# Paced loads in the first loop of an RWKV-6 and GELU kernel: second-step loads, one weight block and one ACT step are moved

## The chip, the cores and the metric

The kernel runs on one core of a Trainium2 chip. The metric is the device time of one execution in microseconds (us). Before the change three runs took 575.78, 577.08 and 580.18 us; the median is 577.08 us. The engines are TensorE (PE, with PEld for its weight loads), VectorE (DVE), ScalarE (ACT), GpSimd (POOL) and SyncE (SP), which here only issues DMAs.

## The reference

RWKV-6 attention on 4 batches, 8 heads, 768 steps and head size 48, then an exact GELU MLP on the 3072 x 384 result.

```python
for t in range(S):                       # S = 768, state is 48 x 48 per head
    kt, vt, rt, wt = (k[:, :, t], v[:, :, t], r[:, :, t], w[:, :, t])
    cur = np.einsum('bhd,bhe->bhde', u[None] * kt, vt)
    y[:, :, t] = np.einsum('bhd,bhde->bhe', rt, state + cur)
    state = wt[:, :, :, None] * state + np.einsum('bhd,bhe->bhde', kt, vt)
x = y.transpose(0, 2, 1, 3).reshape(3072, 384)
h = x @ w_in                             # 384 x 2048
g = 0.5 * h * (1.0 + erf(h / sqrt(2)))
return g @ w_out                         # 2048 x 384
```

## The kernel before

The work is cut into eight steps x = 0 to 7, each half the sequence (384 time steps) of one batch with all heads. Attention is done in chunks of 64 time steps: products of k and r at doubling distances ("levels" h = 1, 2, 4 to 32) are masked into the matrix `a_sb`, then `kv` products make the states, then `a_sb` times v plus r times the states gives y, which is packed into `xT`. Part of y goes into `xT` by copies of ACT and DVE, part is copied to `ysb` by ACT and moved into `xT` by six small DMAs, three issued by SP and three by ACT (`pack`, L886). The MLP of a step runs while the attention of the next step is prepared, so PE has products of both in its queue. The MLP of step 0 (`first_mlp`, L1079 to L1100) makes 16 blocks f of h = x w_in, three matmuls each, in two PSUM banks in turn; ACT applies the GELU to each block (L1086) and so frees its bank.

The weights arrive as 64-bit floats and are converted on the chip in sixteen blocks, eight of w_in and eight of w_out, each 768 KB: `prepare` does three ACT steps on the raw words (L459, L460, L462), `finish` two DVE steps (L471, L475). `weight_in` loads a block, either in one DMA (L322) or, with `gate`, in thirds (L327). Each gated DMA is preceded by a DVE memset of one column of its target, so that it can't be issued before DVE has come to that point in its queue. `conversion` also issues the load of the block three further on, ungated. `load_second` loads r, k and w of step 1 in eight gated shares of 288 KB (L285, L286), r first, w last. `load_first` loads step 0's r, k, w in six DMAs of 384 KB at the start (L274), and `load_v` follows with v, 584 KB (L278).

The order of the instructions on each engine is the order in which the program issues them: nothing is rescheduled. It is written out by hand in `PLAN`. Each letter of `PLAN[x]` advances one stream by one step. In `PLAN[0]`, which covers the first 40 us or so, "." and "s" are the two halves (units) of step 0's attention, "f" is the attention of step 1, "c" the conversions, "l" the gated loads, "w" the load of v of step 1, "p" two further `prepare`s and "x" three matmuls on zeros that keep PE occupied (`warm`). All loads go through SP's queue in program order. In step 1's attention, the first "f" multiplies u and r on ACT (L524, four activations) and makes the running products of w on DVE (L534); the next one issues the first products on PE (L575).

Of the kernel before, what the change touches and what calls it, by code (L numbers as in the profile page):

```python
# [10 lines left out]
F32 = mybir.dt.float32  # L11
# [25 lines left out]
NC_SP = 8  # L37
HALFWAY = 2
PLAN = {
    0: "l.s....llsl.lssslslss.lc.l.slslls...ssss..lcs.s.s.l.ss..ss..sccs.c.s.llpssslw..cs.ffpccxx",  # L40
    1: (
        "swcs.clc.cs.wccscwcc.csccsw..cwlsccccccsc.cs.swcccc.ccc.s.cwlssccsclcs.cwss.lscccsw.c.cwcw"
        ".s..clw..lw..wwccc..cccc.scc.l.cslfccscfccw.fcffy.w.y..fw....ywyw..yyxxx.wyfxx..x.w..y.fyx"
# [149 lines left out]
def kernel(  # L193
# [9 lines left out]
    nc = tc.nc  # L203
# [12 lines left out]
    io = ctx.enter_context(tc.tile_pool(name="io", bufs=2))  # L216
# [8 lines left out]
    def pair(name):  # L225
        return pools["d"].tile([128, 2, BANK], F32, name=name, tag="d")
# [14 lines left out]
    def bank(name="o_ps", i=None):  # L241
        if i is None:
            i = turns[0]
            turns[0] = 1 - i
        return ps.tile([128, BANK], F32, name=name, tag=f"m{i}")
# [4 lines left out]
    loaded = {}  # L250

    def units_of(x):
        return NPART if x == 0 else 1
# [4 lines left out]
    bufs = [io.tile([128, 3 * NP * T], F32, name=f"rkw{i}", bufs=1) for i in range(2)]  # L258
# [7 lines left out]
    def load_first():  # L266

        t = bufs[0]
        loaded[0] = [None, None]
        size = 3 * NP * T // units_of(0)  # L270
        nc.scalar.dma_start(out=u_sb, in_=u)
        for i, part in ((0, 2), (0, 0), (0, 1), (1, 0), (1, 1), (1, 2)):
            s = slice(i * size + part * size // 3, i * size + (part + 1) * size // 3)
            nc.sync.dma_start(out=t[:, s], in_=rkw[0, :, s])  # L274

    def load_v(x, dma):
        loaded[x][1] = io.tile([128, v.shape[2]], F32, name="v_in", bufs=1)
        dma.dma_start(out=loaded[x][1], in_=v[x])  # L278

    def load_second(dma):  # L280

        loaded[1] = [None, None]
        for i in range(SHARES):
            s = slice(i * 3 * ALL // SHARES, (i + 1) * 3 * ALL // SHARES)
            nc.vector.memset(bufs[1][:, s.start:s.start + 1], 0.0)  # L285
            dma.dma_start(out=bufs[1][:, s], in_=rkw[1, :, s])  # L286
            yield
# [26 lines left out]
    def weight_in(i, gate=False):  # L314

        if i < len(pieces):
            dst, src = pieces[i]
            raws[i] = cv.tile([128, PIECE], I64, name="raw", bufs=AHEAD) if wide else None
            if wide:
                dst = raws[i].rearrange("p (a c) -> p a c", a=dst.shape[1])  # L320
            if not gate:
                nc.sync.dma_start(out=dst, in_=src)  # L322
                return
            for a in range(dst.shape[1]):
                if wide:
                    nc.vector.memset(dst[:, a].bitcast(U32)[:, 0:1], 0)
                nc.sync.dma_start(out=dst[:, a], in_=src[:, a])  # L327
                yield

    load_first()  # L330
    load_v(0, nc.sync)


    zeros = const.tile([128, BANK], BF16, name="zeros")
# [8 lines left out]
    def keep_warm(n, elsewhere=False, n_cols=BANK):  # L343
        if elsewhere:
            t = pair("warm")[:, 0]
        else:
            t = bank("warm")
        for _ in range(n):
            nc.tensor.matmul(t[:, 0:n_cols], lhsT=zeros[:, 0:128], rhs=zeros[:, 0:n_cols], start=True, stop=True)
# [83 lines left out]
    def conversion():  # L433

        i = converted[0]
        if i >= len(pieces):
            return
        converted[0] += 1

        prepare(i + HALFWAY if i > 1 else 0)  # L440
        yield
        if wide:
            yield from finish(pieces[i][0], raws[i], *halfway[i])
        for _ in weight_in(i + 3):
            pass

    def convert():
        for _ in conversion():
            pass

    def prepare(upto):
        if not wide:
            return
        for i in range(len(halfway), min(upto, len(pieces))):
            words = raws[i].bitcast(U32).rearrange("p (a b) -> p a b", b=2)
            lo, hi = words[:, :, 0], words[:, :, 1]
            f = cv.tile([128, PIECE], U32, name="f")
            e = cv.tile([128, PIECE], U32, name="e")
            nc.scalar.activation(out=f.bitcast(F32), in_=hi.bitcast(F32), func=AF.Abs, scale=2.0 ** -112)  # L459
            nc.scalar.activation(out=e.bitcast(F32), in_=lo, func=AF.Identity, scale=2.0 ** -51, bias=two)  # L460
            sign = e.bitcast(F16).rearrange("p (a b) -> p a b", b=2)[:, :, 1]
            nc.scalar.activation(out=sign, in_=hi.bitcast(F32), func=AF.Copy, scale=2.0 ** -100)  # L462
            halfway.append((f, e))

    def finish(dst, raw, f, e):

        nc.vector.tensor_scalar(out=f, in0=f, scalar1=3, scalar2=None, op0=ALU.logical_shift_left)  # L471
        yield
        yield
        f, e = (z.rearrange("p (a c) -> p a c", a=dst.shape[1]) for z in (f, e))
        nc.vector.tensor_tensor(out=dst.bitcast(U32), in0=f, in1=e, op=ALU.add)  # L475
# [3 lines left out]
    def attention(x, unit):  # L479
# [20 lines left out]
        def transposed_sums(o, e, n):  # L500
            nc.vector.tensor_reduce(out=fine_sb[:, e, 0:n].rearrange("p a n -> p (a n)"),  # L501
                                    in_=kx[:, o:o + n * n_m].rearrange("p (m j) -> p m j", j=32),
                                    axis=mybir.AxisListType.X, op=ALU.add, apply_transpose=True)
# [7 lines left out]
        if x >= 2:  # L511
            for q in range(qs):
                m_q = slice(q * T // FINE, (q + 1) * T // FINE)
                nc.vector.scalar_tensor_tensor(out=kx[:, 0:n_u].rearrange("p (a m) -> p m a", a=FINE)[:, m_q],
                                               in0=r4[:, m_q], scalar=u_sb[:, q:q + 1], in1=k4[:, m_q],
                                               op0=ALU.mult, op1=ALU.mult)
            yield
            transposed_sums(0, 0, FINE)
            yield
        else:  # L520

            rus = [kx[:, b * Q * T:(b + 1) * Q * T] for b in parts]
            for q in range(qs):
                nc.scalar.activation(out=rus[q // Q][:, q % Q * T:(q % Q + 1) * T], in_=r[:, q * T:(q + 1) * T], func=AF.Copy,  # L524
                                     scale=u_sb[:, q0 + q:q0 + q + 1])
            rucs = [ru.rearrange("p (i c t) -> p i c t", c=2, t=C) for ru in rus]


# [381 lines left out]
        else:  # L910
# [22 lines left out]
            for turn in range(2):  # L933
                ysb = ysb_of() if turn == 0 else ysb
                a = ys[turn][1][:, :, 0:NI * C].rearrange("p b (q i t) -> p b q i t", q=Q, t=C)
                for z in range(2):
                    s = slice(z * G, z * G + D)
# [9 lines left out]
        if split:  # L947
            for c, copy in enumerate((nc.scalar.copy, nc.vector.tensor_copy)):
                for z in range(2):
                    s = slice(z * G, z * G + D)  # L950
                    copy(out=xT[s, 0:Q, :].rearrange("p q (i c t) -> p (q i) c t", c=2, t=C)[:, :, c, :],
                         in_=ys[0][0][c][s, 0:NI * C].rearrange("p (i t) -> p i t", t=C))
# [3 lines left out]
        for b in reversed(range(np_)):  # L956
            for q in reversed(range(Q)):
# [5 lines left out]
                if which < NJ:  # L963
                    for z in range(2):
                        s = slice(z * G, z * G + D)
# [274 lines left out]
    second = load_second(nc.sync)  # L1240
# [8 lines left out]
    def prepare_apart():  # L1249
        for i in range(2, 2 + HALFWAY):  # L1250
            prepare(i)
            yield

    def next_v():
        load_v(1, nc.sync)
        yield

    def warm():
        for _ in range(2):
            keep_warm(3, True)  # L1260
            yield

    def masks_and_sums():
        yield from make_quarter_masks()
        homes()
        yield from h_sums([0])
# [3 lines left out]
    for x in range(NX):  # L1270
        following = attention(x + 1, 0) if x + 1 < NX else iter(())
        if x == 0:
            streams = {
                ".": units[0], "s": units[1], "f": following, "c": pieces_of_w, "w": next_v(), "x": warm(),
                "p": prepare_apart(),
                "l": chain(weight_in(0, True), islice(second, 5), weight_in(1, True), second, weight_in(2, True)),
            }
        else:
            streams = {
                **(mlp(x - 1) if x > 1 else {".": first_mlp()}),  # L1280
                "s": slots, "f": following,
                "l": load(x + 1, nc.sync),
                "x": sums_of_x(x),
                "w": masks_and_sums() if x == 1 else chain(h_sums([1]), o_sums(EARLY, len(FORMS_O))) if x == 2 else iter(()),
                "y": o_sums(0, EARLY) if x == 1 else iter(()),
                "c": pieces_of_w if x == 1 else iter(()),
            }
        for c in PLAN[x]:
            next(streams[c], None)
        for c in ".slxwp" if x == 0 else ".slxwcy" if x == 1 else ".vgeoslxw":  # L1290
            while next(streams[c], streams) is not streams:
                pass
        slots = following
        if x == 1:
            fewer_pairs()
# [63 lines left out]
```

## Time and profile before

| | before |
|---|---|
| median of three runs | 577.08 us |
| the profiled execution | 577.52 us |
| its span | 575.7 us |
| granted TensorE clock | 1.00 |
| PE, DVE, ACT, POOL busy | 551.3, 489.2, 334.1, 106.1 us |
| packets of the queue for instructions (q8) | 58, 0.95 MB |

The span runs from the first to the last instruction on the engines; 1.8 us of the execution lie around it. The first part of the page gives the busy time of each engine, the second cuts the span into 40 slices of 14.4 us with the busy share in tenths. In the order of time, a line gives the start, the duration, the engine, the line of the code, the output and its inputs, the count, and in brackets the idle time of the engine before it and what ended it. "issue" stands where the profile shows nothing that was waited for. SPq and ACTq are DMA issues; their duration is that of issuing. A line's matmul count is twice the program's, since a 32-bit matmul makes two records.

### The profile page before, as it was taken

How to read it: one execution, taken by the hardware profiler on the slowest of the kernel's cores; microseconds unless marked ns; L12 is line 12 of the kernel's file. 1: busy time of each engine (PE TensorE's matmuls, PEld its weight loads, DVE VectorE, ACT ScalarE, POOL GpSimd, SP SyncE). 2: the span in 40 equal slices, each digit the busy share in tenths (PEclk: the TensorE clock that was granted, in tenths of full speed). 3: DMA queues.
4: the chain of work that ended last, by engine and by line, in shares of the span. 5: the costliest groups of instructions: out<-in, count | busy, mean ns of one | idle time of the engine just before them, and what ended most of it. 6: DMA issues, size and time to landing. Idle time of an engine off the chain costs nothing. (4 is left out here: it accounts for less than half of the span.)

```text
span 575.7 us, 17712 instructions
## 1 busy us (share of the span) xinstructions
PE 551.3 (96%) x7412; PEld 491.1 (85%) x7420; DVE 489.2 (85%) x977; ACT 334.1 (58%) x768; POOL 106.1 (18%) x105
## 2 busy tenths in 40 slices
PE   7689999999998999999999999999999999999997
PEld 4576665689998989999898998989898988999997
DVE  7889879999989989798989979799888989755464
ACT  2468995347753677347763477527772478535820
POOL 5100000016200460006400252005500072000000
PEclk9999999999999999999999999999999999999999
DMA  8559742239342782558623593337915384200001
GB/s 303 178 159 370 239 142 87 81 86 154 47 82 64 175 106 36 139 156 131 81 46 114 135 165 44 60 91 159 131 30 135 84 105 62 43 25 30 0 1 41
DMA packets 71646, 62.15 MB, mean 108 GB/s; under 512 B 32912, under 2 KB 56720, under 8 KB 71568
## 3 DMA queue, kind: packets, MB, share of 16 engines
q1 hardware_dynamic: 50112, 45.62, 26.4%
q0 software_dynamic: 21216, 15.34, 20.3%
q8 instruction: 58, 0.95, 0.7%
q14 instruction: 20, 0.16, 0.1%
q10 hardware_dynamic: 240, 0.08, 0.1%
HBM read 36.24 MB, written 4.72 MB: 71 GB/s over the span
## 5 line engine op out<-in xcount | busy, mean ns | idle before, releaser
L1148 POOL DMA_DIRECT2D g<-o_sb x78 | 94.9, 1490 | 370.7 <-ACT g L1117 347.2
L1197 DVE TENSOR_TENSOR g<-g 128x512 f32<-128x512 f32 x112 | 75.1, 688 | 24.3 <-PE o_ps L1073 21.3
L1117 ACT COPY o_sb<-u_ps 128x384 f32<-128x384 f32 (+1 forms) x56 | 25.8, 461 | 67.6 <-PE u_ps L1073 66.2
L1073 PE MATMUL h_ps<-forms_x,w_in_sb 128*128 128x192 f32 x280 | 57.7, 332 | 0.0
L1073 PE MATMUL o_ps<-w_out_sb,g 128*128 128x192 f32 x280 | 50.5, 327 | 0.5 <-DVE g L1197 0.5
L1117 ACT COPY g<-h_ps 128x384 f32<-128x384 f32 x84 | 40.4, 482 | 16.3 <-PE h_ps L1073 14.4
L1073 PEld LDWEIGHTS h_ps<-forms_x,w_in_sb 128*128 128x128 f32 x280 | 46.6, 190 | 2.7 <-ACT g L1117 2.2
L1073 PEld LDWEIGHTS o_ps<-w_out_sb,g 128*128 128x128 f32 x280 | 46.0, 190 | 1.2 <-DVE g L1197 0.8
L1166 ACT ACTIVATE g<-g 128x384 f32<-128x384 f32 x98 | 46.2, 519 | 0.3
L1073 PE MATMUL o_ps<-t,g 128*128 128x192 f32 x224 | 41.4, 328 | 0.1
L726 ACT COPY a_sb<-d 32x320 f32<-32x320 f32 (+5 forms) x108 | 39.3, 364 | 3.6 <-DVE a_sb L784 1.7
L1073 PEld LDWEIGHTS o_ps<-t,g 128*128 128x128 f32 x224 | 36.8, 190 | 0.7 <-PE u_ps L1073 0.3
L1073 PE MATMUL h_ps<-forms_x,s 128*128 128x192 f32 x168 | 35.5, 334 | 0.0
L1073 PE MATMUL h_ps<-xT,w_in_sb 128*128 128x192 f32 x168 | 35.0, 331 | 0.1
L710 PE MATMUL d<-kx,rkw 64*64 64x96 f32 x1152 | 32.0, 248 | 3.0 <-ACT a_sb L726 1.9
L710 PEld LDWEIGHTS d<-kx,rkw 64*64 64x64 f32 x1152 | 25.6, 133 | 9.6 <-issue 4.3
L1084 PE MATMUL h_ps<-xT,w_in_sb 128*128 128x384 f32 x96 | 33.0, 494 | 0.2
L1073 PE MATMUL u_ps<-xT,w_in_sb 128*128 128x192 f32 x168 | 32.5, 328 | 0.1
L1073 PE MATMUL u_ps<-w_out_sb,g 128*128 128x192 f32 x168 | 30.9, 332 | 1.4 <-ACT o_sb L1115 0.8
L1092 PE MATMUL o_ps<-w_out_sb,g 128*128 128x384 f32 x96 | 31.7, 489 | 0.0
L575 PEld LDWEIGHTS d<-rkw 64*64 64x64 f32 x1152 | 19.1, 134 | 14.2 <-issue 8.5
L739 DVE COPY_PREDICATED a_sb<-quarter,d 128x480 f32<-128x480 uint8 (+5 forms) x54 | 23.2, 440 | 8.7 <-PE d L710 7.4
(178 smaller groups left out, 1206.2 us busy)
## 6 DMA issues: line engine op xcount, KB each, us to landing
g<-o_sb POOLq DMA_DIRECT2D x78, 192.0 KB, 4.2
rkw<-in_rkw_dram SPq DMA_DIRECT2D x54, 256.0 KB, 3.7
raw<-in_w_out_dram SPq DMA_DIRECT2D x8, 768.0 KB, 5.4
v_in<-in_v_dram SPq DMA_DIRECT2D x8, 584.0 KB, 4.6
out_dram<-o_sb SPq DMA_DIRECT2D x24, 192.0 KB, 2.1
raw<-in_w_in_dram SPq DMA_DIRECT2D x5, 768.0 KB, 9.2
rkw<-kx SPq DMA_DIRECT2D x72, 48.0 KB, 2.1
rkw<-in_rkw_dram SPq DMA_DIRECT2D x6, 384.0 KB, 6.8
```

The lines of the kernel that those rows point to most:

```text
L575: nc.tensor.matmul(d[half[p], g, n * width:(n + 1) * width], lhsT=kc[half[g], b, i, p], rhs=right(half[g], b, i, p), start=True, stop=True)
L710: nc.tensor.matmul(d[half[p], g, i * 3 * C // 2:(i + 1) * 3 * C // 2], lhsT=kc[half[g], n // NI, n % NI, p], rhs=rx[half[g], 2 * n + p], s ...
L726: nc.scalar.copy(out=at[z, g, first:behind, (a + 1) * h:], in_=d[z, :, :, to] if g == slice(None) else d[z, :, to])
L739: nc.vector.copy_predicated(out=an[:, :, :, :, (a + 1) * h:], mask=mask.to_broadcast(data.shape), data=data)
L1073: nc.tensor.matmul(o, lhsT=lhsT, rhs=rhs, start=start, stop=True, skip_group_check=True)
L1084: nc.tensor.matmul(h_ps, lhsT=w_in_sb[:, f // FI, j, f % FI * 128:(f % FI + 1) * 128], rhs=xT[:, j, :], start=(j == 0), stop=(j == NJ - 1))
L1092: nc.tensor.matmul(o, lhsT=gs[f // FG][:, f % FG, i * 128:(i + 1) * 128], rhs=w_out_sb[:, f, :], start=(f == 0), stop=(f == NF - 1))
L1117: nc.scalar.copy(out=o, in_=z)
L1148: nc.gpsimd.dma_start(out=o, in_=saved[q, t], accum_op=ALU.add)
L1166: nc.scalar.activation(out=o, in_=z, func=AF.Gelu, scale=MINUS.get(h, 1.0))
L1197: nc.vector.tensor_add(o, o, g_block(what[3:5]))
```

## The change

Only the first loop's program changes. The order of PE's matmuls stays. What moves is this:

- v of step 0 is no longer loaded by `load_v` ahead of everything; it is loaded in two gated halves (`first_v`), after w_in's block 0.
- `PLAN[0]` has 20 steps of "l" instead of 17, at other places. The gated order was: block 0, five shares of step 1, block 1, three shares, block 2. It is now: block 0, the two halves of v, five shares, block 1, three shares, block 2, block 3. The last three shares come after the first fence on y, where they came among the products of the levels. All three thirds of block 2 now stand behind the DMAs of `ysb` in SP's queue, with the load of step 1's v between the first and the second; two of them were ahead of these DMAs.
- w_in's fourth block (block 3) is no longer issued in one DMA by the first `conversion`; it is loaded in gated thirds at the end of the list.
- In step 1's attention, u times r gets a step of its own (`if x: yield`), and the plan's extra "f" places it on ACT's queue ahead of the copy to `ysb` and its DMAs. It followed the copies into `xT`.
- The matmuls of `warm` in the first loop have 64 columns instead of 512.

```diff
-    0: "l.s....llsl.lssslslss.lc.l.slslls...ssss..lcs.s.s.l.ss..ss..sccs.c.s.llpssslw..cs.ffpccxx",
+    0: ".s....ls.lssslslss.lc.l.slss.l..lsssls..lcs.s.sl..lss..ss..sccs.c.s.psslfllslw..lcs.llffpccxx",
...
+    def first_v():
+        loaded[0][1] = t = io.tile([128, v.shape[2]], F32, name="v_in", bufs=1)
+        for i in range(2):
+            s = slice(i * v.shape[2] // 2, (i + 1) * v.shape[2] // 2)
+            nc.vector.memset(t[:, s.start:s.start + 1], 0.0)
+            nc.sync.dma_start(out=t[:, s], in_=v[0][:, s])
+            yield
+
     load_first()
-    load_v(0, nc.sync)
...
             yield from finish(pieces[i][0], raws[i], *halfway[i])
-        for _ in weight_in(i + 3):
+        for _ in weight_in(i + 3) if i else ():
             pass
...
                                      scale=u_sb[:, q0 + q:q0 + q + 1])
+            if x:
+                yield
             rucs = [ru.rearrange("p (i c t) -> p i c t", c=2, t=C) for ru in rus]
...
         for _ in range(2):
-            keep_warm(3, True)
+            keep_warm(3, True, 64)
             yield
...
-                "l": chain(weight_in(0, True), islice(second, 5), weight_in(1, True), second, weight_in(2, True)),
+                "l": chain(weight_in(0, True), first_v(), islice(second, 5), weight_in(1, True), second, weight_in(2, True), weight_in(3, True)),
```

## The prediction

> **What bounds the kernel now.** I read the page's first two parts, then the order of time from 0 to 125 us, because nothing after that changes its order of instructions.
>
> ```profile
> PE 551.3 (96%) x7412; PEld 491.1 (85%) x7420; DVE 489.2 (85%) x977; ACT 334.1 (58%) x768; POOL 106.1 (18%) x105
> PE   7689999999998999999999999999999999999997
> q8 instruction: 58, 0.95, 0.7%
> ```
>
> TensorE (PE) is full but for the first three slices, 43 us. That is the first loop, which the change rewrites. 7412 + 7420 = 14,832 PE records over 58 instruction packets are 256 to a packet, so the packets of q8 feed PE's program. That matters here:
>
> ```profile
> 18.12 0.45 PE L575 MATMUL d<-rkw 64*64 64x64 f32 x11 [1.46 <-issue]
> 18.66 0.96 DVE L628 TENSOR_TENSOR rkw<-rkw,tot_sb 128x768 f32<-128x768 f32 x1 [0.45 <-issue]
> 20.03 0.96 DVE L628 TENSOR_TENSOR rkw<-rkw,tot_sb 128x768 f32<-128x768 f32 x1 [0.41 <-PE d L575]
> 22.68 1.39 PE L575 MATMUL d<-rkw 64*64 64x64 f32 x80 [0.61 <-issue]
> 27.45 1.20 DVE L617 TENSOR_TENSOR rkw<-rkw,tot_sb 128x384 f32<-128x384 f32 x2 [0.84 <-issue]
> 33.98 0.86 PE L865 MATMUL y_ps<-a_sb,v_in 64*64 64x64 f32 x44 [1.39 <-issue]
> 37.71 1.59 PE L575 MATMUL d<-rkw 64*64 64x32 f32 x94 [0.57 <-issue]
> ```
>
> The pauses marked "issue" stand in the middle of a run of equal matmuls, where no operand can be missing. Counting PE's records, PE resumes after them at numbers 447, 701, 955, 1211, 1723 and 1979, that is 254 to 256 apart or twice that: it is out of instructions. The times of these boundaries (13.19, 18.12, 22.68, 26.41, 30.25, 33.98, 37.71, 41.31 us) give what one packet takes: 4.93 and 4.56 us from 13 to 23 us, while loads ran at 185 to 270 GB/s (the table by stretches of 4 us), and 3.6 to 3.8 us afterwards, at 43 to 262 GB/s. So traffic may explain part of it, not all. VectorE (DVE) is 88% busy from 10 to 30 us and loses to PE only the 0.45, 0.41 and 0.84 us above and 0.15 us at 23.43: 1.85 us.
>
> ```profile
> 36.10 0.48 ACT L970 COPY ysb<-y_ps 128x384 f32<-128x384 f32 x1 [1.79 <-PE y_ps L894]
> 36.60 1.86 SPq L886 DMA_DIRECT2D xT<-ysb  x3
> 38.57 0.56 SPq L327 DMA_DIRECT2D raw<-in_w_in_dram  x1
> 39.23 1.23 SPq L278 DMA_DIRECT2D v_in<-in_v_dram  x1
> 39.87 2.14 ACT L524 ACTIVATE kx<-rkw,u_sb 128x384 f32<-128x384 f32 x4
> 42.17 0.93 ACT L459 ACTIVATE f<-raw 128x768 f32<-128x768 f32 x1 [0.15 <-DMA raw<-in_w_in_dram]
> 42.58 6.07 PE L1084 MATMUL h_ps<-xT,w_in_sb 128*128 128x384 f32 x18
> 45.15 0.49 ACT L1086 ACTIVATE g<-h_ps 128x384 f32<-128x384 f32 x1
> 48.58 1.60 PE L575 MATMUL d<-rkw 64*64 64x32 f32 x96
> 50.48 0.93 ACT L459 ACTIVATE f<-raw 128x768 f32<-128x768 f32 x1 [1.30 <-DVE w_in_sb L475]
> ```
>
> The hand-over to the second loop: the packed copy ysb, its DMAs into xT, u times r, then the MLP's h products f0, f1, f2 (each 6.07/3 = 2.02 us), for which ScalarE (ACT) converts w_in block by block (about 3 us each). From 42.58 to 120 us PE has no idle time before any group but fractions of a us, so **whatever delays PE after 42.6 us is kept to the end.** ACT sits in front of it: 9.4 to 9.9 of each 10 us busy from 50 to 90. The gelu of f0 stands on ACT behind the three conversions of block 2 (42.17 to 45.13), and f2 needs the PSUM bank which that gelu frees at 45.64. PE reached f2 at 42.58 + 4.05 = 46.6: **1.0 us to spare.**
>
> **The change part by part.**
>
> *Loads of 8 to 30 us.* v no longer goes ungated behind the first six loads; block 0's thirds are gated after the first updates (about 9, 11 and 12.4 us), v's halves follow at about 14.5 and 15.5, five shares of the second r,k,w until 23, block 1 until 26.6. The last three shares and the old 768 KB load at 27.04 leave this stretch. Seven more memsets of 0.06 us on DVE, partly under their neighbours: 0.1 us. Gain: the first two packets could come in 3.7 instead of 4.9 and 4.6 us; in the other direction, block 1 and the shares now run at 22 to 27 us, where the packet took 3.73. Ends: 1.85 us won (all of DVE's waits) and 0.4 us lost. I take 0.4 won, near the small end, since the bytes are moved within the stretch more than taken out of it, and traffic alone didn't set the packet's time. The Trainium skill, "Runtime: NRT & Kernel Launch", section "Instruction fetch mechanics", says that the program streams in 16 KiB blocks of 256 instructions and that crossing a block is mostly hidden; the block size agrees with the trace, the hiding doesn't (1.46 and 1.39 us). By that sentence this part would win nothing, and the sum below would be 0.4 us higher.
>
> *The gap around kv (27 to 33 us).* Packets there took 3.73 to 3.84 us under load and 3.6 without: 0.1 to 0.2 us each, nothing.
>
> *The last three shares.* Their memsets now stand behind the first y fence (33.23 us before), so they are issued at about 33.3 to 34.3; a 288 KB share took 3.7 us at least to land. The first is due for the second part's products (36.9 before), the others for DVE's tot at 38.92. 37.0 to 38.3: just in time, 0 to 0.3 us.
>
> *u times r ahead of ysb.* Four activations, 2.14 us. ACT is free at 34.30 (end of L462), idle for 1.79 us until 36.10. 34.30 + 2.14 = 36.44, so ysb comes 0.34 us later, less the 0.4 won above: 36.0 to 36.4. xT's DMAs, and DVE's L967, which waits for ysb, move with it. With this, u times r is ready when the products want it; the six warm matmuls go from 512 to 64 columns, about 1.3 of their 1.47 us. Together f0 could start up to 1.6 us earlier, if instructions arrive (next boundary 41.31) and xT has landed: 36.6 + 3.4 to 4.8 us.
>
> *Block 2 after xT.* This is where I see the end set. Before, two thirds of block 2 were issued at 31.20 and 31.63, and one at 38.57. Now its first third goes out after xT's six small DMAs, then v of the second part, then the other two. The compiled lists of both kernels show that each DMA takes the next of eight completion counters and its issue waits until that counter's last DMA has landed. In the changed list the second third waits for ACT's first xT DMA and the last third for SP's first. These start at 36.6 and take 3.4 to 4.4 us, so the last third goes out at about 40.6, not 38.57. Landing, bound below: a 256 KB third took 3.5 us from 38.57 with an empty queue, so 44.1. Bound above: it queues behind v, 584 KB, which landed at 44.96 before, and another 1 us of its own: 46.0. I take 45.2, the middle, as v is in front but partly drained. ACT then starts block 2 at 45.2, not 42.17; u times r being out of its way gives it nothing but idle time. Gelu of f0 ends at 45.2 + (45.64 - 42.17) = 48.7, and f2 starts at 48.7, not 46.6: **+2.1 us** (+1.0 to +2.9 by the bounds), whenever f0 started. f3 follows after 2.02 + 1.6 us at 52.3; it needs the gelu of f1, behind block 3 on ACT: 45.2 + 6.6 = 51.8, no further wait. On ACT, block 4 starts at 45.2 + 7.0 = 52.2 against 50.48.
>
> *Block 3 in thirds at the end.* It was loaded at 27.04; now behind block 2, two thirds gated by memsets after DVE's L471 (41.5). Three thirds at 0.7 to 1.0 us each after 45.2 land at 47.5 to 48.2; ACT wants it at 48.7. Covered by block 2's own lateness; without that cover it would cost 2 us by itself, as ACT wanted it at 45.54. All later loads come 1.3 MB later in a queue that moved 390 GB/s from 47 to 53: 3.4 us. Block 4 then lands at about 49 against 52.2, w_out blocks have 7 us (converted 91, used 99). Nothing.
>
> **Sum.** The early gains end in the wait for f2, so they don't add: +2.1 us. The profiled execution took 577.52 us (span 575.7), so 579.6; the runs' median is 0.44 lower, so I write **579.3**.
>
> **The rivals.**
> 1. *The early gain is carried.* If the last third of block 2 lands by 43.1 us (46.6 - 3.47), f2 waits for nothing, and 0.5 to 1.5 us of the early stretch remain: 576.1. For it: 1.5 us of packet pauses and 1.79 us of ACT idle. Against: the counter would have to be free at 39.5, when xT has been under way for 3 us. Chance 0.23.
> 2. *Nothing moves.* Early gain 1 us and block 2 at 44 cancel, within 0.7 us of before: 577.1. Chance 0.15.
> 3. *Slower, and more.* Block 3's last thirds fall behind v and block 2, and ACT waits for them too: block 3 at 50 instead of 48.7 adds 1.3 us, and DVE, whose L471 for block 2 stands in order ahead of the mask copies that free d's buffers, adds up to 1 us: 581.5. Decides from a landing at 49 us. Chance 0.13.
> 4. *The clock.* PE would idle from about 45.7 to 48.7. The longest gap in this trace is 1.5 us, at a granted clock of 1.00 throughout. If it fell to half for the next 3.4 us, that would add 1.7 us: 581.0. "TensorE: Matmul & The Clock Gate" of the Trainium skill, part 1, tells of half clock after an idle window of about 3.4 us; no run here shows it. Chance 0.04.
>
> The forecast itself has 0.45. The range takes in rivals 1 to 4 but for their tails: 575.0 to 582.0. One per cent, 5.8 us, is about what a measurement of this kernel can tell from no change; no case reaches it alone, so within 1% has 0.93, faster 0.02, slower 0.05.
>
> **What would show it.** In the new profile: ACT's first conversion after xT's copies waits for DMA raw until 44 to 46; the first h_ps group on PE breaks after two products, with an idle time before the third released by ACT g; the x11 and x44 groups' pauses shrink, if pacing works; ysb starts at 36.0 to 36.5. I am wrong if block 2 lands by 43, or if PE's idle time after 60 us swallows 2 us.

## The result and the profile after

The changed kernel took 580.3 us (median of 22 runs, 576.26 to 585.59), the kernel before 577.3 us in 22 runs beside them: ratio 1.0046, 95% interval 1.0026 to 1.0066. (The ratio is worked out over the fast runs and is not the quotient of the two medians, which here is 1.0052.) The forecast was 579.3 in a range of 575.0 to 582.0, within 1%. So the number held. The way to it held in part: one step came out on the spot, one that I called nothing was not, and what the rival with the smallest chance names, the clock at half speed, was at work in most executions (15 of 22).

The profiled execution of the changed kernel took 578.78 us, its span 577.0, at a granted clock of 1.00. The first two parts of its page:

```profile
PE 550.2 (95%) x7420; PEld 490.3 (85%) x7420; DVE 489.4 (85%) x982; ACT 332.8 (58%) x768; POOL 106.0 (18%) x105
...
PE   7769999999998999999999999999999999999997
```

PE did 1.1 us less work than before (the six warm matmuls went from 1.47 to 0.35 us) in a span 1.3 us longer. From the order of time, the lines of PE and DVE that answer to the pauses before (all line numbers are 7 to 9 higher than before):

```profile
16.18 0.45 PE L584 MATMUL d<-rkw 64*64 64x64 f32 x11 [0.68 <-issue]
...
20.85 1.40 PE L584 MATMUL d<-rkw 64*64 64x64 f32 x80 [0.68 <-issue]
...
25.90 1.20 DVE L626 TENSOR_TENSOR rkw<-rkw,tot_sb 128x384 f32<-128x384 f32 x2 [1.10 <-issue]
...
30.07 0.62 PE L833 MATMUL kv_ps<-v_in,kx 64*64 64x48 f32 x28 [1.19 <-issue]
...
33.52 0.86 PE L874 MATMUL y_ps<-a_sb,v_in 64*64 64x64 f32 x44 [1.36 <-issue]
...
38.07 1.60 PE L584 MATMUL d<-rkw 64*64 64x32 f32 x94 [1.26 <-issue]
...
42.07 1.26 PE L584 MATMUL d<-kx,rkw 64*64 64x64 f32 x68 [1.47 <-issue]
```

The x11 group starts at 16.18, not 18.12, after 0.68 us of waiting instead of 1.46: the early part is faster. But a new pause stands in the middle of the kv products (x28), the pause before x94 has doubled (0.57 before), and x68 ahead of f0 waits for its program too. The hand-over:

```profile
32.63 2.11 ACT L531 ACTIVATE kx<-rkw,u_sb 128x384 f32<-128x384 f32 x4
...
35.64 0.48 ACT L979 COPY ysb<-y_ps 128x384 f32<-128x384 f32 x1 [0.90 <-PE y_ps L903]
...
43.27 4.14 PE L1093 MATMUL h_ps<-xT,w_in_sb 128*128 128x384 f32 x12
...
45.08 0.91 ACT L466 ACTIVATE f<-raw 128x768 f32<-128x768 f32 x1 [5.72 <-DMA raw<-in_w_in_dram]
...
48.02 0.49 ACT L1095 ACTIVATE g<-h_ps 128x384 f32<-128x384 f32 x1
...
48.56 2.20 PE L1093 MATMUL h_ps<-xT,w_in_sb 128*128 128x384 f32 x6 [1.15 <-ACT g L1095]
...
50.69 1.60 PE L584 MATMUL d<-rkw 64*64 64x32 f32 x96
...
52.06 0.92 ACT L466 ACTIVATE f<-raw 128x768 f32<-128x768 f32 x1
```

ACT waits 5.72 us for block 2 and starts it at 45.08; the gelu of f0 follows at 48.02, and f2 (the x6 group) at 48.56, where it was at 46.6 before. The x96 group stands at 50.69 against 48.58: PE is 2.11 us behind. Aligned instruction by instruction, it is still 2.0 us behind at 77 us, 1.59 at 83 us, 1.1 around 400 us and 1.57 in the last products.

**A second thing the runs say.** Each run gives its mean granted clock, and that falls in steps of 0.003: one step is a stretch of 3.41 us at half clock. The profiled executions of both kernels have none of these. The 22 runs of the changed kernel have 1.64 per execution (none in 7 of 22, three in 9), the 92 runs of the kernel before that stand beside the experiments 0.45 (none in 63). A straight line through each kernel's runs gives

| | runs | mean us | stretches per execution | line: us without any + us per stretch |
|---|---|---|---|---|
| before | 92 | 578.1 | 0.45 | 577.3 + 1.78 |
| changed | 22 | 580.5 | 1.64 | 578.1 + 1.45 |

So of the 2.4 us between the means about 0.8 is there at full clock; 1.19 more stretches at 1.45 to 1.78 us are 1.7 to 2.1 us. (The two make a little more than the whole, since the lines are fitted.) The 0.8 is rough: by the scatter of the runs about the lines its standard error is 0.6 us. The 92 runs were taken in four groups, whose own lines start at 576.8 to 577.6 us. And the 22 runs of before that stand beside the changed ones have a mean of 577.5, 3.0 us lower; there is no clock for each of them.

### The profile page after: what moved, and what is told of

The parts are those of the page before. It is cut to its first block, busy times and chain, and to the rows that moved or that the text cites. A ratio compares the mean times of both kernels' runs of the same rounds, so it can differ in the third digit from the quotient of the medians.

```text
span 577.0 us, 17734 instructions
## 1 busy us (share of the span) xinstructions
PE 550.2 (95%) x7420; PEld 490.3 (85%) x7420; DVE 489.4 (85%) x982; ACT 332.8 (58%) x768; POOL 106.0 (18%) x105
## 3 DMA queue, kind: packets, MB, share of 16 engines
q1 hardware_dynamic: 50288, 45.62, 26.7%
## 5 line engine op out<-in xcount | busy, mean ns | idle before, releaser
L1206 DVE TENSOR_TENSOR g<-g 128x512 f32<-128x512 f32 x112 | 75.0, 687 | 24.3 <-PE o_ps L1082 21.4
L1082 PEld LDWEIGHTS h_ps<-forms_x,w_in_sb 128*128 128x128 f32 x280 | 46.6, 190 | 2.7 <-ACT g L1126 2.1
```

Source lines behind the costliest of these rows:

```text
L1082: nc.tensor.matmul(o, lhsT=lhsT, rhs=rhs, start=start, stop=True, skip_group_check=True)
L1206: nc.vector.tensor_add(o, o, g_block(what[3:5]))
```

## The experiments

Two theories at first. A: the late block 2, as forecast, makes the loss. B: the stretches at half clock make most of it. In the last column a line as above; it is left out where it is not steady. Its standard error is 0.4 to 1.1 us, so two kernels that differ there by less than 1 us can't be told apart by it.

| kernel | runs | median | ratio to before | stretches | line at none |
|---|---|---|---|---|---|
| changed | 22 | 580.3 | 1.0046 [1.0026, 1.0066] | 1.64 | 578.1 |
| e1: changed, warm 512 | 12 | 580.5 | 1.0044 [1.0022, 1.0066] | 0.67 | 579.4 |
| e2: changed, block 2 early | 11 | 581.1 | 1.0042 [1.0017, 1.0068] | 1.36 | |
| e3: before, warm 64 | 12 | 577.7 | 1.0008 [0.9979, 1.0037] | 1.17 | 577.0 |
| e4: before, block 2 late | 7 | 583.4 | 1.0081 [1.0045, 1.0116] | 2.14 | |
| e5: changed, v last | 8 | 581.0 | 1.0063 [1.0037, 1.0088] | 1.12 | 578.7 |
| e6: changed, blocks in time, warm 512 | 12 | 579.9 | 1.0046 [1.0023, 1.0069] | 0.83 | 578.5 |
| e7: before, u times r ahead | 12 | 577.9 | 1.0015 [0.9990, 1.0041] | 0.67 | 576.5 |
| e8: before, early loads paced | 6 | 580.5 | 1.0072 [1.0043, 1.0101] | 1.50 | 578.8 |
| e9: changed, 14 matmuls on zeros | 6 | 586.1 | 1.0104 [1.0059, 1.0149] | 1.50 | 584.2 |
| e10: e7, 14 matmuls on zeros | 12 | 583.2 | 1.0069 [1.0038, 1.0100] | 0.67 | 581.9 |
| e11: before, block 3 late | 12 | 578.9 | 0.9995 [0.9964, 1.0026] | 0.58 | 577.9 |
| e12: e8 and e11 together | 10 | 580.1 | 1.0046 [1.0024, 1.0068] | 0.90 | 580.0 |

### e1 and e3: the width of the warm matmuls

```diff
-            keep_warm(3, True, 64)      # e1, in the changed kernel
+            keep_warm(3, True)
-            keep_warm(3, True)          # e3, in the kernel before
+            keep_warm(3, True, 64)
```

> The changed kernel with one part undone: the six warm matmuls of the first loop have 512 columns again. Theory A (the time is lost to the late landing of w_in's block 2, and nothing else): nothing gained, since PE waits for its program at 42.07 anyway; ratio to before as for the changed kernel, 1.003 to 1.007, ACT's first conversion after the xT copies again at about 45. Theory B (in many executions TensorE's granted clock falls, because PE has too little to do between 36 and 48 us; the executions of the changed kernel had mean clocks of 0.990 to 1.000, those at 0.991 took about 582 us, those at 1.000 about 578): with 1.3 us more PE work just there the low clocks become rare, and the median falls from 580.3 to about 578.5, ratio about 1.002.

> The kernel before with one part of the change alone: warm matmuls of 64 columns. Theory A: nothing, ratio 0.999 to 1.001, since u times r (39.87 to 42.01) sets the start of the products and not PE. Theory B: PE is idle for 1.3 us more from 39.6, so low clocks (0.991 to 0.997) appear in part of the executions and the ratio is 1.002 to 1.005.

Both ways the narrow matmuls go with more stretches (0.67 to 1.64, 0.45 to 1.17). The line at none is lower with them (579.4 to 578.1, 577.3 to 577.0), but not by more than its errors allow. The ratios don't move: 1.0044 beside 1.0046, and 1.0008 beside 1. So theory A's ratios were met and theory B's were not, though the counts went B's way. Whether the matmuls on zeros save or cost time can't be told from these runs.

In the traces the busy share of PE over 3.41 us falls, between 36 and 43 us, to no less than 0.82 (before) and 0.70 (e1), but to 0.57 (changed) and 0.56 (e3) with 64 columns. None of these four profiles lost the clock there, though. The one stretch at half clock in e3's profile runs from 13.5 to 16.9 us, where its program is still that of before; e10 and e11, which have the loads of before too, lost theirs at the same place. Only e5, with 64 columns, lost it after 36.4 to 39.8 us. That the width brings stretches on is therefore what the counts say; the traces of e1 and e3 don't show it.

### e2 and e4: block 2 early in the changed kernel, late in the one before

```diff
-        for _ in weight_in(i + 3) if i else ():           # e2
+        for _ in weight_in(i + 3 if i else 2):
...
-..., second, weight_in(2, True), weight_in(3, True)),
+..., second, weight_in(3, True)),
...
-... "ssss..lcs.s.s.l.ss..ss..sccs.c.s.llpssslw..cs.ffpccxx",      # e4
+... "ssss..lcs.s.s.l.ss..ss..sccs.c.s.pssslwll..cs.ffpccxx",
```

In e2 block 2 is loaded in one DMA by the first conversion at 25 us. In e4 all its thirds go behind the DMAs of `ysb`, the last two behind v, and nothing else changes.

> The changed kernel, but the first conversion issues the load of block 2 (768 KB, one DMA, at about 25.5 us, where the kernel before issued block 3), and only block 3 is loaded in thirds behind ysb's DMAs. Theory A: ACT converts block 2 as soon as it has copied xT (about 39.5), f2 follows f1 without a wait, and the 2.1 us on PE at 48.6 are gone; ratio 0.997 to 1.001, a fast profile's span 575 to 576. Theory B alone: the warm matmuls are still short, but the wait for f2 is gone, so fewer low clocks than in the changed kernel. A rival, that the load in the gap slows the program's packets around kv: the pauses before kv and y (1.19 and 1.36 us) grow by 0.5 us each or more, and the ratio stays above 1.002.

> The kernel before with one part alone: all three thirds of block 2 stand behind ysb's DMAs on SP, with v between the first and the second, as in the changed kernel; block 3 stays in one DMA at 27 us. Theory A: block 2 lands at 45 to 46, f2 starts 2 to 2.8 us later than before (46.6), the ACT chain 1.6 to 2.2 us later, ratio 1.003 to 1.004, span 577.3 to 578. If late landing were harmless, 1.000. Theory B says nothing against that, but adds low clocks if PE's wait for f2 is what lowers them (ratio 1.005 and more).

In e2's order of time, f0 to f2 run through, and the wait has moved on to f3:

```profile
33.94 0.87 PE L874 MATMUL y_ps<-a_sb,v_in 64*64 64x64 f32 x44 [1.91 <-issue]
...
43.61 6.07 PE L1093 MATMUL h_ps<-xT,w_in_sb 128*128 128x384 f32 x18
...
49.13 0.92 ACT L466 ACTIVATE f<-raw 128x768 f32<-128x768 f32 x1 [2.80 <-DMA raw<-in_w_in_dram]
...
52.44 6.07 PE L1093 MATMUL h_ps<-xT,w_in_sb 128*128 128x384 f32 x18 [1.23 <-ACT g L1095]
```

Block 3, which the lateness of block 2 had covered, is now what ACT waits for, and f3 starts at 52.44 against 52.22 in the changed kernel. It is not the only reason: f0 itself starts 1.03 us later than before (42.58), since PE waited 1.91 us at y for its program (1.36 in the changed kernel) and then lost the clock from 34.66 to 38.08. Before kv the wait was 0.92, so of the rival's two pauses one grew. Nothing is won: 1.0042, where theory A had 0.997 to 1.001. In e4 the loss is larger than in the change, and than theory A had it (f2 2 to 2.8 us later, 1.003 to 1.004): f2 starts 5.0 us later than before. Of e4, PE's line for f2 in the order of time:

```profile
51.61 4.21 PE L1084 MATMUL h_ps<-xT,w_in_sb 128*128 128x384 f32 x6 [4.14 <-ACT g L1086]
```

and its table by stretches (from and to, us, busy time and count of PE, PEld, DVE, ACT and POOL, granted clock, DMA share, GB/s):

```profile
46.80:50.20 3.40, 0.67 (x3) 0.05 (x1) 1.08 (x2) 1.98 (x3) 0.00 (x0) 1.00 1.04 389
50.20:53.60 3.40, 1.99 (x3) 1.17 (x4) 3.37 (x5) 3.34 (x5) 0.00 (x0) 0.50 1.04 374
53.60:57.00 3.40, 3.40 (x52) 1.93 (x53) 2.37 (x4) 2.20 (x4) 0.00 (x0) 0.50 1.00 360
```

PE is busy for 0.67 of 3.4 us while it waits for block 2 (ACT's first conversion 48.19, 6.0 us later than before), and the next 6.8 us run at half clock. Here one can see theory A's wait become theory B's stretch. Late block 2 alone is therefore enough for a loss; in the changed kernel it was milder (45.08).

### e5: v behind the blocks

```diff
-... "psslfllslw..lcs.llffpccxx",
+... "psslfllsl..lcs.llllwffpccxx",
```

> The changed kernel with one thing moved: the load of step 1's v is issued behind blocks 2 and 3, not between the first and the second third of block 2. Theory A (the landing of block 2 sets the kept loss; v's 584 KB in front of its last two thirds are part of it): the last third lands at 44.0 to 44.5 us, not 45.05, ACT's first conversion of block 2 starts there, and f2 starts at 47.5 to 48.0 after 0.3 to 0.6 us of waiting instead of 1.15; PE is then 1.2 to 1.5 us behind before at 60 us, not 2.1. At full clock about 0.5 to 0.7 us less than the changed kernel. Theory B (the loss seen in the median is mostly 3.41 us windows at half clock, drawn anew in each execution): the same number of such windows as the changed kernel, 1.2 to 2.0 per execution, so that the ratio to before stays at 1.003 to 1.005 and a gain of 0.6 us is hardly seen. If the third waits for the counter of SP's first xT DMA and not for v's transfer, the landing stays at 44.7 to 45.1 and neither moves.

ACT's first conversion of block 2 starts at 44.56, 0.5 us earlier than in the changed kernel, just above the 44.0 to 44.5 expected; v was a part of the lateness, a small one, for with v out of the way the issue of the last third was late (held until about 41 us, by the profile for DVE's tot, and done at 41.29). f2 runs on without a wait, but at 49.42: f0 itself started at 44.30, since this execution had 6.8 us at half clock from 39.82 on. By the ratio nothing is won.

### e6: no wait left at f2 and f3

```diff
-        for _ in weight_in(i + 3) if i else ():
+        for _ in weight_in(i + 3 if i else 2):
...
-            keep_warm(3, True, 64)
+            keep_warm(3, True)
...
-... "psslfllslw..lcs.llffpccxx",
+... "psslfllsl..lcs.llwffpccxx",
```

> The changed kernel with block 2 in one DMA issued by the first conversion (about 25 us), so that it's there long before ACT wants it; block 3 in gated thirds where block 2's thirds were, the load of v behind them; and the warm matmuls at 512 columns again. It keeps the paced early loads and u times r ahead of the copy to ysb. Theory A: neither f2 nor f3 waits; ACT's first conversion of block 2 follows the copies into xT at 40 to 41 us, block 3 lands at 44 to 45 against about 45.5 wanted. PE is 0 to 1 us behind before at 60 us, and the fit at zero windows gives 577.0 to 578.0. The 768 KB of block 2 run at 25 to 28 us, which takes back the gap around kv: the program packet there takes 5 us or more, and DVE's pause at kv stays at 1 to 1.5 us. Theory B: with 512 columns and without the idle time at f2 there are 0.4 to 0.9 windows per execution, so the ratio is 0.999 to 1.002; with 1.2 or more windows theory B's account of what brings them on is wrong.

As expected neither f2 nor f3 waits. Yet f0 starts at 44.86, 2.3 us later than before, and the ratio is 1.0046. Theory B had 0.999 to 1.002 for the 0.83 stretches that it counted rightly. The line at none, 578.5, is above A's 577.0 to 578.0 by less than its error. The loss sits earlier; PE's lines in the order of time:

```profile
25.87 2.84 PE L584 MATMUL d<-rkw 64*64 64x64 f32 x96 [2.11 <-DVE raw L326]
...
32.21 0.62 PE L833 MATMUL kv_ps<-v_in,kx 64*64 64x48 f32 x28 [1.12 <-issue]
...
44.86 6.07 PE L1093 MATMUL h_ps<-xT,w_in_sb 128*128 128x384 f32 x18
```

Between the first two starts lie 6.34 us for one packet of the program. The trace records each of these packets: this one began 3.97 us after PE had entered the last one. Block 2's 768 KB had been issued at 25.43, just ahead of it. And in the stretch of 3.41 us from 22.2, with a busy share of 0.35, the clock was lost for the next one (25.56 to 28.98).

### e7: u times r ahead of the copy, alone

```diff
-... "llpssslw..cs.ffpccxx",
+... "llpssfslw..cs.ffpccxx",
...
+            if x:
+                yield
```

> The kernel before with one part of the change: u times r is a step of its own on ACT, ahead of the copy to ysb. Loads and warm matmuls as before. Forecast by the prediction's step: ACT fills its 1.79 us pause with 2.1 us of activations, ysb starts 0.3 to 0.5 us later (36.4 to 36.6), xT's DMAs land 0.3 to 0.5 us later, f0 starts where it did or 0.3 later (42.6 to 42.9), and PE has up to 1 us to spare before f2, so nothing is kept: ratio 0.999 to 1.001. ACT's first conversion of block 2 moves from 42.17 to about 40.5, so f2 has more to spare. Theory B: windows as before, 0.3 to 0.8 per execution. If this part alone costs 1 us or more, or brings 1.2 windows or more, the late block 2 isn't the only source of the base loss.

1.0015 [0.9990, 1.0041]: no difference that these runs can tell. (The line at none, 576.5, stands beside 576.8 for the runs of before in the same group.) ACT's first conversion of block 2 moved only to 41.24, since it then waits for the data. PE is 0.42 us ahead of before at 60 us, but it is 1.2 ahead already at 18 us, where the two programs are the same: so much do two executions differ by the waits for program packets.

### e8, e11 and e12: paced early loads and the gap around kv, alone and together

```diff
-    0: "l.s....llsl.lssslslss.lc.l.slslls...ssss..lcs.s.s.l.ss..ss..sccs.c.s.llpssslw..cs.ffpccxx",
+    0: ".s....ls.lssslslss.lc.l.slss.l..lsssls..lcs.s.sl..llllss..ss..sccs.c.s.llpssslw..cs.ffpccxx",   # e8
...
+    def first_v(): ...                   # e8, as in the change; load_v(0, nc.sync) goes
...
-        for _ in weight_in(i + 3):       # e11: block 3 in thirds at the end
+        for _ in weight_in(i + 3) if i else ():
```

e12 has both edits.

> The kernel before with only the early loads paced: v of step 0 in two gated halves behind block 0, block 0 later, five shares, block 1, then the last three shares straight after it; block 3 still in one DMA by the first conversion, two thirds of block 2 ahead of ysb's DMAs, 512 columns, u times r where it was. Theory A (the early gain is real but is lost again to program packets and then hidden behind the hand-over): DVE is 1 to 1.8 us ahead of before at 25 us, 0 to 1 us at 38 us, 0 to 0.5 us at 60 us; no wait at f2. At full clock 576.4 to 577.4, ratio 0.998 to 1.000. If the early gain were carried whole, 575.5 and ratio 0.997. Theory B: 0.3 to 0.8 windows per execution, like before, since PE does the same work in nearly the same times.

> The kernel before with block 3 alone moved: from one DMA at the first conversion (27 us) to thirds at the end of the list, behind the load of step 1's v. So it has the gap in the loads around kv, and block 2 lands as before. The prediction's steps: the gap is worth 0.1 to 0.2 us (packets there took 3.73 to 3.84 us under load and 3.6 without), and block 3 late, uncovered, costs about 2 us. By the counters and the transfers in front of it (v of 584 KB and 768 KB of its own) the last third lands at 46.5 to 48.5, and ACT wanted it at 45.54: ACT starts block 3 1.0 to 3.0 us late and PE is that much later at f3, 50.1 + 1 to 3, kept to the end: ratio 1.002 to 1.005. The other theory of the gap, from the version without it (a packet asked for at 28.9 us had to wait for 3.5 us behind loads, where 1.1 is the least): the packets asked for at 26.4 and 30.25 start 1.1 us after their boundary and take 3.45 to 3.6 us, not 3.73 to 3.84; that is no more than 0.4 us in all, since before asks for them where little is queued. Windows 0.3 to 1.0, as PE idles at f3.

> The kernel before with the paced early loads (as in the version that did only that) and block 3 moved from 27 us to thirds at the end of the list, so that the loads pause around kv. Against the version without that move it takes 768 KB out of the queue at 26.7 us. The packet theory (a program packet waits in its DMA engine behind loads issued before it was asked for): there the packet asked for at 28.9 us started 3.47 us later, and PE waited 3.83 us for it; now it starts 1.1 to 2.2 us later, PE waits 1.4 to 2.5 us, ysb starts at 34.8 to 36.0, not 37.7, and f0 at 41.8 to 42.8, not 44.95. If something else held that packet (the three shares issued at 25.3 us, or the program's own place in the order), its start stays 3 us or more behind its boundary. Block 3 then lands at about 48.5 and costs 1 to 2 us at f3, as when it alone was moved (f3 at 52.1). Sum: PE 0.5 to 1.8 us behind the profile of before at 60 us, the fit at zero windows 576.8 to 578.2, windows 0.3 to 0.9, ratio 0.999 to 1.003: the early gain pays for the late block 3 and no more.

e8 fell outside what either theory allowed. At 26 us PE is 1.9 us ahead of before, at 42.6 it is 2.4 behind. PE's lines in the order of time:

```profile
28.88 0.62 PE L831 MATMUL kv_ps<-v_in,kx 64*64 64x48 f32 x28 [0.36 <-issue]
...
34.80 0.86 PE L872 MATMUL y_ps<-a_sb,v_in 64*64 64x64 f32 x44 [3.83 <-issue]
```

and the table by stretches, with the columns as above:

```profile
28.90:32.30 3.40, 2.07 (x128) 1.93 (x128) 2.90 (x19) 3.37 (x4) 0.00 (x0) 1.00 0.92 336
32.40:35.80 3.40, 1.00 (x57) 1.00 (x58) 1.65 (x11) 0.00 (x0) 0.00 (x0) 1.00 0.54 203
35.80:39.20 3.40, 3.40 (x81) 3.40 (x79) 1.07 (x4) 0.48 (x1) 0.00 (x0) 0.50 0.02 5
```

After 28.88 the loads run at 336 GB/s, and the next packet begins only at 32.35, 3.47 us after PE entered the last one: PE is out of program for 3.83 us, and pays again with a stretch at half clock, in which the products with the states take 3.79 us. e12 takes one thing away, the 768 KB of block 3 at 26.7 us, and the pause halves (order of time, PE and ACT):

```profile
33.04 0.86 PE L872 MATMUL y_ps<-a_sb,v_in 64*64 64x64 f32 x44 [1.91 <-issue]
...
35.69 0.48 ACT L977 COPY ysb<-y_ps 128x384 f32<-128x384 f32 x1 [2.88 <-PE y_ps L901]
...
42.18 6.41 PE L1091 MATMUL h_ps<-xT,w_in_sb 128*128 128x384 f32 x18
```

ysb comes at 35.69 instead of 37.73 and f0 at 42.18 instead of 44.95, both in the ranges expected of the packet theory. So the loads were what held the packet. On the loads of before, the same move (e11) leaves the packet as it was: asked for at 26.63, begun at 27.73, 1.10 us later, as before (26.41 and 27.50). In e11 the late block 3 makes f3 wait 1.15 us on PE; the ratio is 0.9995 [0.9964, 1.0026], an interval that has room for 1.15 us (0.2%), so the runs neither show this loss nor exclude it.

e12's sum failed: 1.0046 and a line at none of 580.0, not 0.999 to 1.003 and 576.8 to 578.2. Its trace is 0.5 to 0.8 us behind before from 51 to 400 us, and then loses 1.3 us at one place, where ACT waits 2.13 us for a small DMA instead of 0.70 (order of time, ACT):

```profile
404.26 0.48 ACT L1124 COPY o_sb<-u_ps 128x384 f32<-128x384 f32 x1 [2.13 <-DMA g<-o_sb]
```

The same step stands in the profiles of e1, e2, e5 and e6, not in those of the changed kernel, e8, before, e3, e7 and e11. All five have the paced loads, but one execution each doesn't settle whether these bring it on: e3 and e11, with the loads of before, fall back by 1.2 and 1.3 us between 200 and 300 us. So most of e12's loss stays unexplained.

### e9 and e10: matmuls on zeros in the waits

```diff
+    def fill(t, n):
+        for _ in range(n):
+            nc.tensor.matmul(t[:, 0:BANK], lhsT=zeros[:, 0:128], rhs=zeros, start=True, stop=True, skip_group_check=True)
...
+            if x == 0 and not warm:
+                fill(d[:, 0], 1 if len(bs) == 1 else 3)
...
+            if x == 0 and b == 0:
+                fill(kv_ps[:, 0], 2)
...
+                if split:
+                    fill(y[0], 4)
```

> The changed kernel plus 14 matmuls on zeros in the first loop, each 128x512 and about 0.25 us by the warm group of six in 1.47 us: one ahead of each of the six products from the third level on, two ahead of each kv, four ahead of the second y, all written into the tile that the next product overwrites. Nothing else differs. They stand where PE waits anyway (for DVE's updates, ACT's kx, or the next program packet). Theory B (stretches of 3.41 us at half clock follow a 3.41 us stretch in which PE was busy half the time or less, and most of the change's loss in the median is these): with PE's busy share raised by 0.1 to 0.3 around 20 to 34 us the changed kernel's 1.64 windows per execution fall to 0.2 to 0.8, and the mean falls by 1.2 to 2 us to 578.5 to 579.3; the fit at zero windows stays within 0.5 us of the changed kernel's 578.1. Theory A (late block 2 and program packets alone): windows don't matter, 14 matmuls of 0.25 us add 0 to 1 us: ratio 1.0045 to 1.006. If the number of windows stays at 1.2 or more, what brings them on isn't PE's busy share in this loop.

> The kernel before with u times r ahead of the copy to ysb and the same 14 matmuls on zeros as in the kernel with them on the changed one. u times r ahead alone gave 576.5 at zero windows and 0.67 windows per execution, the kernel before in the same call 576.8 and 0.32. Theory B: 0 to 0.2 windows, so a mean of 576.3 to 577.0 and a ratio of 0.997 to 1.000, the version that would beat both by a little. If the matmuls delay the products instead (program boundaries come 28 records earlier, and the first kv stands behind two of them), PE is 0.5 to 1.5 us later at 30 us, and the ratio is 1.000 to 1.003.

Both failed. Stretches stayed at 1.50 and 0.67, and the time rose by 5 to 6 us, more than the 14 matmuls (3.4 us) take. In e9 PE was busy for 0.75 or more of each 3.41 us from 10.5 to 37.8 us, and no clock was lost there; but everything behind came later, block 2 with it (ACT's first conversion at 47.77), PE waited 3.02 us at f2, and lost the clock after that. In e10 the one lost stretch followed 9.9 to 13.4 us (share 0.52), where no filler stood. That agrees with theory B on what brings a stretch on, and refutes my idea that filling these waits is free.

## Why the prediction was right, and where it was not

**Program packets, early pacing: mis-sized.** I took 0.4 us won. (It never entered the sum, which is 2.1 alone. So my remark that without it the sum would be 0.4 us higher was wrong.) The transposes `kt_ps`, next after the products of the levels, start at 28.0 us in the mean of five profiles with the old loads (27.1 to 28.7) and at 26.65 in six with the paced ones (26.2 to 27.3; e6, with its extra load, left out): 1.35 us won, inside my ends of 1.85 won and 0.4 lost but near the other one. Three of the five (e3, e4, e11) had a stretch at half clock on the way; against the other two, 27.6 in the mean, it is 1.0 us. I said that early gains don't add since they end in the wait for f2; they ended sooner, in the packets: 0.7 us is left at ysb (36.0 against 35.3 in the three of the six whose clock was full there; 36.1 in all six) and nothing at f0.

**The gap around kv: this step failed.** I priced it at nothing, from packets of before that took 3.73 to 3.84 us. That was right of the kernel before (e11). With the paced loads it isn't: there PE waits 3.83 us at y without the gap (e8), 1.91 in e12, and in the changed kernel 1.36, after another 1.19 at kv for a packet that stood behind block 1. I had read the packets' times against the traffic of their own stretch; what counts is how much stands in the queue at the moment when the packet is asked for.

**The last three shares.** DVE's tot waited 0.67 us, where I had 0 to 0.3. The profile names xT's DMA, but the last share landed at 39.11, just ahead of tot at 39.23. PE lost nothing by it directly. But the late shares held SP as well: the first third of block 2 was not issued before the counter of the second share was free (landed 38.35, issue 38.41), nor v before that of the third (39.11, 39.18). The forecast has neither wait.

**u times r ahead of ysb:** ysb was forecast at 36.0 to 36.4 and came at 35.64. It waited for PE, not for ACT. Alone it does nothing that shows (e7). The 1.3 us saved by the narrow warm matmuls don't arrive: the x68 group behind them waits 1.47 us for a packet, as I had allowed ("if instructions arrive").

**Block 2 after xT: right in place and size, in part by another way.** Last third landed at 45.05 (forecast 45.2), conversion at 45.08 (45.2), gelu's start 48.02, f2 at 48.56 (48.7), PE 2.11 us behind (2.1). What held the issues was not what I said. The two xT DMAs whose counters the second and the last third wait for had landed at 39.47 and 39.30, before SP came to them. The second third's issue began at 39.60 and ended only at 41.14; the profile puts 1.2 us of this down to DVE's tot, and that had itself waited for the last share. The last third followed at 41.23 (forecast 40.6). Nor did this set the landing, it seems: from 39.9 to 45.4 us the DMA engines are 0.85 busy or more, and the first third, v, the second and the last third land one behind the other at 42.32, 43.74, 44.40 and 45.05. So the term that held is the queue of my upper bound, with v in front; that the middle of two bounds came out within 0.2 us is luck.

"Kept to the end" was wrong by 0.5 us: an h group of 18 matmuls took 6.38 us from 77.90 in the kernel before, since it had to wait for gelus, and 5.97 in the changed one. In the span 1.3 us are left and in the line at none 0.8.

**Block 3: right.** Covered by block 2, and once that cover is gone (e2) it is what f3 waits for; e11's trace gives 1.15 us of PE's time for it, not 2.

**The rivals.** Rival 4, the clock, had 0.04, with PE's idle time at f2 as its place and 1.7 us as its price. The price per stretch was right (1.45 to 1.78). The chance wasn't: I looked for one long gap in a profile whose clock was full, but the runs before already had 0.45 stretches each, which one profile can't show. The place was not borne out either: in the changed kernel's profile the clock stayed full after the 1.15 us at f2. By the counts of e1 and e3 the narrow warm matmuls have a part in it. By the profiles the waits for program have one too: in e2, e6, e8 and e12, all with the paced loads, the clock was lost after stretches that hold such a wait between 22 and 36 us. So 579.3 (by its own terms 579.2) was met, with less at full clock than I had (0.8 by the lines, 1.3 to 1.6 by the two profiles, not 2.1) and with half-clock stretches in place of the rest. That these came to about what was missing is luck. "TensorE: Matmul & The Clock Gate" of the Trainium skill, part 1, gives the free-running window of about 3.4 us and the half rate; both agree with the runs (3.41 us, 0.50).

**What stays open.** Which place brings the changed kernel's stretches on can't be read from its profile, which has none. (Over any 3.41 us after the first 8 us its lowest busy shares are 0.51 from 21.4 us on and 0.57 from 38.7 us on.) And no part alone carries the loss: late block 2 is enough by itself (e4, 1.0081), but without it the changed kernel is no faster (e2, e6). All seven kernels with the paced loads and no fillers lie at 1.0042 to 1.0072; with the old loads, and block 2 where it was, the three are at 0.9995 to 1.0015. The paced loads thus belong to the cause, though they bring PE to kv 1.0 to 1.35 us earlier. No kernel that was tried beat the one before.

## What to carry to other kernels

A kernel whose program streams in while loads are running has a second customer on its DMA queues: look where the program's packets are asked for (pauses marked "issue", about 256 instructions apart) and keep large loads from being issued just ahead of them. A change that wins early time on a full engine moves these moments too, so ask what stands in the queue at the new ones. And read the clock of many runs, not of one profile: here six matmuls on zeros, 1.1 us of PE's time, went with 0.7 to 1.0 fewer stretches at about 1.5 us each, and the time stayed the same.

## What the runs showed of the hardware

**A program packet's time has three parts.** From PE's entry into one packet, which I take for the moment when the next is asked for, to the next packet's beginning: about 1.1 us at the least (1.05 to 1.13 in eleven of the fourteen profiles, for one from 30.07 to 31.18 in the changed kernel, with 5 GB/s in all on the DMA engines), 1.2 to 2.9 us in most others up to 40 us, 3.47 and 3.97 us at worst there, behind the loads of e8 and e6. The packets asked for at 41 to 43 us, when several loads of a block are queued, begin 2.5 to 4.8 us later in twelve profiles, in the kernel before too (41.30 to 45.66); PE has the longer h products then and doesn't run dry. After the beginning come 0.9 to 1.6 us for the 16 KB, and 1.1 to 1.6 us from its end to PE's first instruction where PE stood still. That makes 3.45 us at best (30.07 to 33.52 in the changed kernel), while 96 of the small products with their weight loads, 192 instructions, last 1.6 us. The Trainium skill, "DMA: Bandwidth & Descriptors", section "Queues, rings and completion order", says that an engine takes turns between its queues packet by packet. By that a queue full of loads should hold up another queue's packet by about one packet; the traces show 2.9 us more than the least in e6, and up to 3.7 us more after 41 us, so here it isn't the whole of it.

**Half clock follows half work, not only idleness.** The stretches lie on a grid of 3.41 us whose phase differs between executions. In fourteen profiles, up to 70 us, the stretches of the grid at full clock, by PE's busy share in them:

| busy share | stretches | the next one at half clock |
|---|---|---|
| up to 0.50 | 7 | 7 |
| 0.50 to 0.55 | 6 | 3 |
| 0.55 to 0.60 | 7 | 1 |
| 0.60 to 0.66 | 22 | 0 |
| above 0.66 | 201 | 0 |

In the stretch of e6 with a share of 0.35 the longest idle time was 2.11 us, 1.81 of it inside the stretch, and e2, e4, e10, e11, e12 and e3 lost the clock after stretches that were 44 to 54% busy. "TensorE: Matmul & The Clock Gate" of the Trainium skill, part 1, tells of half clock after an idle window; here half a window's idleness was enough. So a loop that waits often and briefly can lose the clock, and by the phase of the grid it does in some executions and not in others.
